# Both hidden-dimension transforms by seven half-size products per pair of row blocks, behind all query and key products

## The chip, the cores and the metric

The kernel runs on one core of one Trainium2 chip. Its time is device time in microseconds (us). Before the change three runs took 851.29, 848.71 and 847.14 us; the median is 848.71 us. One more execution was profiled: it took 850.56 us, and the profile's span of it is 848.9 us.

A core has a matrix engine (PE in the profile; PEld is its weight load), a vector engine (DVE), an activation engine (ACT), GpSimd (POOL), and SP, which here only issues transfers. All of them run their own instruction list in order.

## What is computed

Two token mixers are computed from the same 2048x512 input `x` and blended by a gate per row. The first is the real part of a two-dimensional discrete Fourier transform, as four dense products; the second is attention in a sliding window of 256 with 32 heads of 16.

```python
a = einsum("bsd,ed->bse", x, dft_hid_re)          # 2048x512 by 512x512
b = einsum("bsd,ed->bse", x, dft_hid_im)
fnet = einsum("ts,bse->bte", dft_seq_re, a) - einsum("ts,bse->bte", dft_seq_im, b)
q, k, v = split(x @ wqkv)                         # 32 heads of 16
p = softmax(where(0 <= i - j < 256, q @ k.T / 4, -1e9))
attn = (p @ v) @ wo
g = sigmoid((x * gate_w).sum(-1))
out = g * fnet + (1 - g) * attn
```

All is float32. A dense product is made of three matrix products on split operands: each operand is a high part plus a low part, and high by high, high by low and low by high are added (`TERMS`). The high part is a cast on ACT, the low part a subtraction on DVE (raw minus high).

## The kernel before

**Two streams on PE.** Attention walks over 128 visits `n` (8 pairs of head groups `G` by 16 query blocks). In a visit stand two score products of `s_pair` (L363; DVE then takes a row maximum of each from PSUM, L367), two transposed score products of `t_pair` (L422; ACT takes the exponential, L425, and POOL masks two triangles of it, L427 and L431), and every fourth visit the product with v of four blocks, `pv` (L445). Scores, transposed scores and `pv` share two PSUM buffers (`ps_a`), so a score product waits until DVE has read the one before it. Between the attention's instructions `fill` (L1070) puts steps of the dense stream, in equal numbers for all visits: those steps that are left are spread over the visits that are left.

**The dense stream.** `dense` (L635) yields one step at a time. `halves64` (L534) works through a list of `Part`s. A step is two matmuls (L527): one on partitions 0 to 63 for the running part, and one on partitions 64 to 127 for the part that began `DELAY` = 6 steps earlier; both have 64 rows of weights and 512 columns and share the matrix array. A part of q, k, v, a or b has 12 steps, and a part of the sequence transform (c) 24. `halves64` has 1,950 steps: 70 parts of 12, 46 of 24, and 6. Each part's result is evicted when its second half ends.

**What sets the order.** PE, ACT, DVE, POOL and SP all run in the order in which the code emits (`manual_schedule`). An action can be put off by a number of steps: `after(n, ...)`, and jobs run one every fourth step (`job`, L159). The parts stand in `order` (L722 to L774): some v parts with q and k of group 0, then q and k of group 1 (8 parts), then 16 parts of b (`ab_part(1, sb)`), then q and k of groups 2 and 3 (16 parts), then 16 parts of a. Each q or k part is evicted into `home`, three buffers used in turn (`hl_tile`), and stored to DRAM as 768 KB (`qk_evict`, L274). Each b block, and the first four blocks of a, goes to DRAM as 256 KB (`ab_evict`, L339); the other twelve blocks of a are split in PSUM straight into their places in SBUF. At the start of the c parts `to_c` (L836) loads the four stored blocks of a back and splits them. Later, c parts with b load its 16 blocks by `next_b` (L804).

## Time and profile before

| what | value |
|---|---|
| median of three runs | 848.71 us |
| profiled execution, its own time | 850.56 us |
| span of it in the profile | 848.9 us |
| granted clock of PE, mean | 0.996 |
| DMA moved in the span | 168.80 MB, mean 199 GB/s |
| steps of `halves64` on PE (L527) | first at 33.5 us, last at 697.2 us |
| stores of q and k (`qk_scr<-home`) | 12.5 us to 258.6 us |
| evictions of b (L342); of a into SBUF (L103) | 120.3 to 264.8 us; 271.0 to 318.5 us |
| last `pv` of the attention (L445) | starts at about 698 us |

The profile's page gives busy times by engine, and the trace answers more narrow questions: groups of instructions by line, waits, single instructions in order of time, and the busy time of each engine in any stretch. One cycle below means four visits of the attention, from the start of one `pv` to the start of the next; it holds 8 pairs of score products and about 58 dense steps.

### The profile page before, as it was taken

Reading aid. Unit: us, or ns where it says so; the run is one execution under the profiler, and the core shown is the slowest. Engines: PE = TensorE matmul, PEld = TensorE weight load, DVE = VectorE, ACT = ScalarE, POOL = GpSimd, SP = SyncE. Lnnn points to the kernel's source line nnn. Section 1 sums busy time; section 2 is a strip of 40 time slices with the busy share of each in tenths; the row PEclk is TensorE's granted clock in tenths of the full one; section 3 lists DMA queues with packets and bytes.
Section 4 is the critical chain, followed back from the end, with each engine's and each line's share of the span. In section 5 each row is a group of like instructions: output and inputs, shape, how many; then the busy total and the mean of one; then the engine's idle time right before and its main releaser. Section 6 shows DMA issues by size and latency. Waiting matters only on the chain.

```text
span 848.9 us, 19774 instructions
## 1 busy us (share of the span) xinstructions
PE 821.5 (97%) x7298; PEld 654.2 (77%) x7298; DVE 531.1 (63%) x1504; ACT 418.0 (49%) x814; POOL 365.0 (43%) x683
## 2 busy tenths in 40 slices
...
GB/s 341 279 207 163 283 247 182 169 181 261 302 263 211 144 124 197 138 175 155 169 142 181 153 192 187 226 231 228 237 230 184 168 180 224 261 213 190 179 111 50
DMA packets 109344, 168.80 MB, mean 199 GB/s; under 512 B 34240, under 2 KB 43968, under 8 KB 109248
## 3 DMA queue, kind: packets, MB, share of 16 engines
...
q8 instruction: 57, 0.93, 0.5%
...
HBM read 107.74 MB, written 59.51 MB: 197 GB/s over the span
## 4 chain that ended last, share of the span: by engine, by line
PE 76%; DMA 8%; DVE 7%; issue 5%; ACT 3%; POOL 1%; SPq 1%; ACTq 0%; DVEq 0%; POOLq 0%
PE d L527 41%; PE o L445 9%; PE dc L580 8%; PE s L363 6%; PE t L1012 5%; PE t L422 4%; DVE junk L367 3%; PE d L567 3%; DMA ring<-qk_scr 2%; DMA raw<-ci 2%; ACT pt L425 1%; DVE lo L156 1%; DMA o_scr<-ev 1%; DVE big L140 1%; DMA stage<-ab_scr 1%
## 5 line engine op out<-in xcount | busy, mean ns | idle before, releaser
L367 DVE CUSTOM_DVE_ANT_0 junk<-s,mask 128x384 f32<-128x384 f32 (+2 forms) x512 | 271.9, 531 | 198.0 <-PE s L363 186.9
L527 PE MATMUL d<-big,hi 64*128 64x512 f32 x1920 | 344.5, 394 | 0.0
L427 POOL TENSOR_SCALAR_AFFINE_SELECT pt<-pt 128x256 f32<-128x256 f32 x256 | 112.3, 439 | 359.4 <-ACT pt L425 280.8
L425 ACT ACTIVATE pt<-t 128x768 f32<-128x768 f32 (+2 forms) x256 | 197.6, 772 | 123.8 <-PE t L422 121.4
L527 PEld LDWEIGHTS d<-big,hi 64*128 64x128 f32 x1920 | 195.5, 187 | 27.0 <-issue 0.6
L527 PE MATMUL d<-big,lo 64*128 64x512 f32 x960 | 206.2, 395 | 0.0
L527 PE MATMUL d<-hi,big 64*128 64x512 f32 x672 | 132.3, 392 | 0.0
L363 PE MATMUL s<-ring,ring 48*128 48x384 f32 (+2 forms) x512 | 99.5, 357 | 12.4 <-DMA ring<-qk_scr 3.7
L527 PEld LDWEIGHTS d<-big,lo 64*128 64x128 f32 x960 | 100.6, 187 | 13.2 <-issue 0.2
L155 ACT CAST hi<-raw 128x512 fp32r<-128x512 f32 x142 | 87.1, 618 | 30.0 <-PE d L527 15.2
L156 DVE TENSOR_TENSOR lo<-raw,hi 128x512 fp32r<-128x512 f32 x110 | 85.4, 777 | 12.9 <-ACT hi L155 12.9
L431 POOL TENSOR_SCALAR_AFFINE_SELECT pt<-pt 128x256 f32<-128x256 f32 x224 | 92.9, 415 | 0.0
L580 PE MATMUL dc<-big,hi 128*128 128x512 f32 x284 | 91.7, 392 | 0.0
L422 PE MATMUL t<-ring,ring 50*128 50x384 f32 (+2 forms) x512 | 87.8, 330 | 1.0 <-ACT pt L425 0.5
L445 PE MATMUL o<-pt,vt 128*32 128x384 f32 (+2 forms) x1408 | 84.3, 386 | 3.9 <-DVE ml L367 3.7
L527 PEld LDWEIGHTS d<-hi,big 64*128 64x128 f32 x672 | 76.8, 186 | 7.4
L363 PEld LDWEIGHTS s<-ring,ring 48*128 48x128 f32 x512 | 53.7, 185 | 37.3 <-issue 10.4
L527 PE MATMUL d<-lo,big 64*128 64x512 f32 x336 | 80.4, 392 | 0.0
L445 PEld LDWEIGHTS o<-pt,vt 128*32 128x32 f32 x1408 | 42.0, 110 | 49.7 <-issue 27.6
L422 PEld LDWEIGHTS t<-ring,ring 50*128 50x128 f32 x512 | 50.7, 185 | 14.5 <-ACT pt L425 2.1
L156 POOL TENSOR_TENSOR lo<-raw,hi 128x512 fp32r<-128x512 f32 x32 | 43.0, 1356 | 40.8 <-ACT hi L155 40.5
L580 PEld LDWEIGHTS dc<-big,hi 128*128 128x128 f32 x284 | 52.3, 188 | 8.7 <-issue 0.2
...
## 6 DMA issues: line engine op xcount, KB each, us to landing
ring<-qk_scr SPq DMA_DIRECT2D x128, 192.0 KB
...
```

The source lines that it names most:

```text
L155: jobs.append(lambda c=c: nc.scalar.copy(hi[:, c], raw[:, c]))
L156: jobs.append(lambda c=c: (nc.gpsimd if FIN else nc.vector).tensor_sub(lo[:, c], raw[:, c], f(hi[:, c])))
L363: nc.tensor.matmul(ps[:, h, :w], ring[0][r, p, j * P:j * P + P], ring[1][r, p, k0:k0 + w], start=True, stop=True)
L367: mark("dve", nc.vector.tensor_tensor_reduce(out=junk[:, :w], in0=ps[:, h, :w], in1=mask[:, WIN - w:], scale=1.0, scalar=3e38, op0=OP.add, ...
L422: nc.tensor.matmul(ps[:, h, :w], ring[1][r, p, q0:q0 + P], ring[0][r, p, q0:q0 + w], start=True, stop=True)
L425: nc.scalar.activation(pt[:, ph, :w], ps[:, :, :w], AF.Exp, scale=-1.0)
L427: nc.gpsimd.affine_select(a, a, pattern=[[0, 2], [1, P]], compare_op=OP.is_ge, fill=0.0, base=0, channel_multiplier=-1)
L431: nc.gpsimd.affine_select(a, a, pattern=[[0, 2], [-1, P]], compare_op=OP.is_gt, fill=0.0, base=0, channel_multiplier=1)
L445: nc.tensor.matmul(o[32 * j:32 * j + 32, (a - 4 * c) * P:(e - 4 * c) * P], v[:, kb % 4, 32 * j:32 * j + 32], PT[G * NB + kb][:, j, (a - kb ...
L527: nc.tensor.matmul(o.ps, lhs[r], rhs[r], start=start, stop=end and o.left == 0, skip_group_check=True)
L580: nc.tensor.matmul(ps, w[a][:, i % 8 * 128:i % 8 * 128 + 128], ab[SC[i]][:, b], start=i == ends[0] and a + b == 0, stop=i == ends[1] and a ...
L1012: nc.tensor.matmul(ps, o[:, a, c], fin(n, b, c), start=start and c == 0 and a + b == 0, stop=c == 1 and a == 1, skip_group_check=True)
```

## The change

**a and b together.** For a pair of row blocks (t, t+4) and the two halves of the features, a and b are the columns of one 256x512 by 512x1024 product: a two-by-two block product in which a's and b's weights are the two column halves. It is computed by seven products instead of eight (the Winograd form of Strassen's scheme). `pair` lists them as seven parts of 6 steps, eight pairs in all, in place of the 32 parts of 12 steps. The sums of weight blocks (`w_sum`, four of them, 1024 columns each) and of input blocks (`x_sums`, four of 256 columns per pair) are made on POOL, the splits of the sums on ACT with DVE or POOL (`w_split`, `x_split`), and the results are put together by additions behind the evictions (`keep`, `p5_mid`, `p6_end`, `fourth`, `p7_end`, `p5_end`). The input is loaded again in another layout (`xp`).

**Order.** q and k of groups 1, 2 and 3 (24 parts) now stand one behind the other ahead of all of a and b; the loads and products of the gate (`gate_load`, `gates`) move into parts 9 to 23. `halves64` has 38 parts of 12, 56 of 6, 46 of 24, and 6 steps: 1,902.

**Places.** Weight blocks and input sums reuse the places of the input tiles. All of b and twelve blocks of a now go through DRAM; `reload` brings the twelve back around the start of the c parts, and only 10, 14, 11 and 15 (`place`) are split into SBUF at once. `SC`, the order in which the c parts take the blocks of a and b, follows from that.

```diff
+AHEAD = 216
+SC = 10, 14, 9, 13, 8, 12, 0, 11, 15, 4, 1, 5, 2, 6, 3, 7
...
-    STAGE = []
-
-    def load_ab(i, sc, into):
-        if not STAGE:
-            t = const.tile([P, 6, 512], F32, name="stage", tag="home")
-            STAGE.extend(t[:, k] for k in range(6))
-        STAGE.append(STAGE.pop(0))
-        raw = STAGE[-1]
+    stage = [f(home[:, 512 * k:512 * k + 512]) for k in range(6)]
+
+    def flat(t):
+        return t.rearrange("p a s -> p (a s)")
+
+    def load_ab(i, sc, dst, into, wait=SPLIT_AB):
...
+        stage.append(stage.pop(0))
+        raw = stage[-1]
         ld_pool(raw, ab_scr[i][sc])
 
         def cast():
-            t = into[sc] = big.tile([P, 2, 512], F32R, name="big")
-            nc.scalar.copy(t[:, 0], raw)
-            after(3, nc.vector.tensor_sub, t[:, 1], raw, f(t[:, 0]))
-        after(SPLIT_AB, cast)
-
-    def ab_evict(i, sb, ps, dst=None):
-        if dst is None:
-            t = ev.tile([P, 512], F32, name="ev")
-            nc.scalar.activation(t, ps, AF.Copy, scale=1.0 if i == 0 else -1.0)
-            after(STORE, ld, ab_scr[i][sb], t)
-        else:
-            split_psum(dst[:, 0], dst[:, 1], ps)
-
+            into[sc] = dst
+            nc.scalar.copy(dst[:, 0], raw)
+            after(3, nc.vector.tensor_sub, dst[:, 1], raw, f(dst[:, 0]))
+        after(wait, cast)
...
-        def __init__(self, end, parts=1, load=None):
-            self.end, self.left, self.load, self.ps, self.r = end, 2 * parts, load, None, None
+        def __init__(self, end, parts=1, load=None, mid=None):
+            self.end, self.left, self.load, self.ps, self.r, self.mid = end, 2 * parts, load, None, None, mid
+
+    class Straight(list):
...
-            if o.left:
+            if o.left == 2 and o.mid:
+                o.mid(o)
+            elif o.left:
...
-        second = [(p, i) for g in groups for p in [g[-1], *g[:-1]] for i in range(p.n)]
+        second = [(p, i) for g in groups for p in (g if isinstance(g, Straight) else [g[-1], *g[:-1]])
+                  for i in range(p.n)]
...
-        def ab_part(i, sb, pre=None):
-            def end(o):
-                if i == 0 and sb >= 4:
-                    ab[sb] = big.tile([P, 2, 512], F32R, name="big")
-                ab_evict(i, sb, o.ps, ab.get(sb) if i == 0 else None)
-            return Part(Out(end), lambda: row_ops(sb, W["ab", i]), pre=pre)
...
+        order = [q02, k02, v_part(6), v_part(7), v_part(8), q03, v_part(9), k03, *(v_part(sb) for sb in range(10, 16))]
+        order += [p for ss in range(4) for p in qk_parts(1, ss)]
+        order += [p for ss in range(4) for g in (2, 3) for p in qk_parts(g, ss)]
...
+        def split_to(n, hi, lo, raw, scale=1.0):
+            def high(c):
+                if scale == 1.0:
+                    nc.scalar.copy(hi[:, c], raw[:, c])
+                else:
+                    nc.scalar.activation(hi[:, c], raw[:, c], AF.Copy, scale=scale)
+
+            def low(c):
+                if scale == 1.0:
+                    nc.vector.tensor_sub(lo[:, c], raw[:, c], f(hi[:, c]))
+                else:
+                    nc.vector.scalar_tensor_tensor(lo[:, c], raw[:, c], scale, f(hi[:, c]),
+                                                   op0=OP.mult, op1=OP.subtract)
+            for k, c in enumerate(HALVES):
+                after(n + 6 * k, high, c)
+                after(n + 6 * k + 3, low, c)
...
+        def w_sum(n, op, dst, a, b):
+            def go(c):
+                getattr(nc.gpsimd, op)(RAWS[dst][:, c], RAWS[a][:, c], RAWS[b][:, c])
+            for k, c in enumerate(HALVES):
+                after(n + 2 * k, go, c)
...
+        def x_load(p):
+            RAWS["x", p] = load_raw(xp[p])
+
+        def x_sums(p):
+            r = RAWS["s", p] = raw_tile()
+            a11, a12, a21, a22 = quarters(RAWS["x", p], 4)
+            s3, s1, s2, s4 = quarters(r, 4)
+            nc.gpsimd.tensor_sub(s3, a11, a21)
+            nc.gpsimd.tensor_add(s1, a21, a22)
+            nc.gpsimd.tensor_sub(s2, s1, a11)
+            nc.gpsimd.tensor_sub(s4, a12, s2)
+
+        XSPOTS = [(k, 2) for k in range(4)] + [(k, 3) for k in range(2)]
...
+        def x_split(n, p, k):
+            def go():
+                t = tiles[p, k] = XT[XSPOTS[(4 * p + k) % 6]]
+                m = 256 if k == 3 else 512
+                raw = (RAWS["x", p][:, :512], RAWS["s", p][:, :512],
+                       RAWS["s", p][:, 512:], RAWS["x", p][:, 768:])[k]
+                nc.scalar.copy(t[:, 0, :m], raw)
+                after(3, (nc.gpsimd if k in (1, 2) else nc.vector).tensor_sub, t[:, 1, :m], raw, f(t[:, 0, :m]))
+            after(n, go)
+
+        def prepare():
+            t = AHEAD
+            for n, k, src in ((-190, "i1", wi[1]), (-178, "i0", wi[0]), (-166, "r0", wr[0]), (-100, "r1", wr[1])):
+                after(t + n, load_w, k, src)
+            w_split(t - 144, "b11", "r0", None)
+            w_sum(t - 144, "tensor_sub", "i1", "i0", "i1")
+            w_sum(t - 139, "tensor_add", "i0", "i0", "r0")
+            w_sum(t - 132, "tensor_add", "r0", "i1", "r0")
+            w_split(t - 127, "t3", "i1", None)
+            w_split(t - 105, "t1", "i0", ((0, 1), 0), -1.0)
+            w_split(t - 93, "t2", "r0", ((2, 3), 0))
+            after(t - 84, load_w, "n1", wi[1])
+            w_split(t - 60, "b21", "r1", ((0, 1), 1))
+            w_sum(t - 46, "tensor_sub", "r1", "r1", "r0")
+            w_split(t - 38, "t4", "r1", ((2, 3), 1))
+            w_split(t + 2, "b22", "n1", None, -1.0)
+            for p in range(8):
+                b = t + 42 * p - 42
+                after(t - 38 if p == 0 else t + 14 if p == 1 else b - 8, x_load, p)
+                after(b + (20 if p == 0 else 29 if p == 1 else 22), x_sums, p)
+                for k, n in enumerate((30, 35, 40, 38) if p == 1 else (26, 31, 39, 35)):
+                    x_split(b + n, p, k)
...
+        def pair_rows(p):
+            t = p % 4 + p // 4 * 8
+            return t, t + 4
+
+        def x_ops(p, k, quarter, w):
+            t = tiles[p, k]
+            a = [t[:, h, 256 * quarter:256 * quarter + 256] for h in range(2)]
+            return [(a[i][:, c * 128:c * 128 + 128], WO[w][j][:, c * 512:c * 512 + 512])
+                    for c in range(2) for i, j in TERMS]
+
+        def pair(p):
+            t1, t2 = pair_rows(p)
+            U, V = [], []
...
+            def p5_mid(o):
+                nc.vector.tensor_add(V[0], o.ps, V[0])
+
+            def p6_end(o):
+                nc.vector.tensor_add(U[0], o.ps, U[0])
+
+                def fourth():
+                    nc.gpsimd.tensor_add(V[0], V[0], U[0])
+                    after(STORE, ld, ab_scr[1][t2], V[0])
+                after(3, fourth)
+
+            def place(t, k):
+                ab[t] = XT[((2, 3), (3, 3))[k]] if p == 6 else XT[XSPOTS[(26 + k) % 6]]
+                return ab[t]
+
+            def p1_end(o):
+                if p < 6:
+                    e = ev.tile([P, 512], F32, name="ev")
+                    nc.scalar.copy(e, o.ps)
+                    after(STORE, ld, ab_scr[0][t1], e)
+                else:
+                    d = place(t1, 0)
+                    split_psum(d[:, 0], d[:, 1], o.ps)
+
+            def p7_end(o):
+                e = ev.tile([P, 512], F32, name="ev")
+                nc.vector.tensor_add(e, o.ps, U[0])
+                if p < 6:
+                    after(STORE, ld, ab_scr[0][t2], e)
+                else:
+                    d = place(t2, 1)
+                    after(3, nc.scalar.copy, d[:, 0], e)
+                    after(6, nc.vector.tensor_sub, d[:, 1], e, f(d[:, 0]))
+
+            def p5_end(o):
+                e = ev.tile([P, 512], F32, name="ev")
+                nc.vector.tensor_add(e, o.ps, U[0])
+                after(STORE, ld, ab_scr[1][t1], e)
+
+            o1 = Out(shortly(p1_end), 2, mid=keep(U))
+            o7 = Out(shortly(p7_end), 2, mid=keep(V))
+            o5 = Out(shortly(p5_end), 2, mid=shortly(p5_mid))
+            o6 = Out(shortly(p6_end))
+            return Straight(Part(o, lambda args=args: x_ops(p, *args), 6) for o, *args in
+                            ((o1, 0, 0, "b11"), (o7, 1, 0, "t3"), (o5, 1, 1, "t1"), (o6, 2, 0, "t2"),
+                             (o1, 0, 1, "b21"), (o7, 3, 0, "t4"), (o5, 2, 1, "b22")))
...
-        order += [p for ss in range(4) for p in qk_parts(1, ss, (PRE.get((1, ss)), None))]
-        order += [ab_part(1, sb, do(*AB1.get(sb, ()))) for sb in range(16)]
-        for g in (2, 3):
-            order += [p for ss in range(4) for p in qk_parts(g, ss, (PRE.get((g, ss)), None))]
-        order += [ab_part(0, sb, do(*AB0.get(sb, ()))) for sb in range(16)]
-        groups = [order[:4], *(order[i:i + 3] for i in range(4, len(order), 3))]
...
+        def reload():
+            w = [XT[dk, ss] for ss in range(2) for dk in range(4)]
+            x = [XT[XSPOTS[(28 + k) % 6]] for k in range(4)]
+            casts = [-5] * 6
+            for n, sc, dst in ((27, 9, w[0]), (29, 13, w[1]), (31, 8, x[1]), (34, 12, w[2]), (37, 0, w[3]), (46, 4, w[4]),
+                               (50, 1, w[5]), (54, 5, x[0]), (60, 2, w[6]), (64, 6, w[7]), (68, 3, x[3]), (72, 7, x[2])):
+                at = max(n - 29, casts[-6] + 5)
+                casts.append(n)
+                after(at, load_ab, 0, sc, dst, ab, n - at)
...
+        for p, k, fn in ((6, 1, pieces.load), (7, 0, lambda: (reload(), pieces.load())), (7, 1, pieces.split),
+                         (7, 3, pieces.load), (7, 4, pieces.split), (7, 6, pieces.load)):
+            pairs[p][k].pre = fn
+        groups = [order[:4], *(order[i:i + 3] for i in range(4, 31, 3)), order[31:35], order[35:], *pairs]
...
-        def to_c():
-            for sc in range(4):
-                after(8 * sc, load_ab, 0, sc, ab)
-
-        c_groups[0][0].mid[12] = to_c
...
+        "xp": x.reshape(2, 2, 4, P, 2, 2, P).transpose(0, 2, 6, 1, 4, 5, 3).reshape(8, P, 1024),
```

**What it moves on POOL.** First POOL's instructions before, from the stretch with the parts of b: the two masks of each transposed score product (`pt`), `o_mul` (L475) once in four visits, and a load of the gate's input (L70).

```order
L475 TENSOR_TENSOR ev_2024<-ots_312,ev_2024 128x512
L427 AFFINE_SELECT pt_2162<-pt_2162 128x2x128
L431 AFFINE_SELECT pt_2162<-pt_2162 128x2x128
L427 AFFINE_SELECT pt_2255<-pt_2255 128x2x128
L431 AFFINE_SELECT pt_2255<-pt_2255 128x2x128
L70 DMA raw_2301<-x 128x512 x2
```

And now POOL's list in one of the pairs (lines are those of the changed kernel: L420 and L424 are the masks, L468 is `o_mul`).

```order
L748 TENSOR_TENSOR raw_4019<-raw_3862 128x256
L749 TENSOR_TENSOR raw_4019<-raw_3862 128x256
L750 TENSOR_TENSOR raw_4019<-raw_4019,raw_3862 128x256
L751 TENSOR_TENSOR raw_4019<-raw_3862,raw_4019 128x256
L420 AFFINE_SELECT pt_3989<-pt_3989 128x2x128
L424 AFFINE_SELECT pt_3989<-pt_3989 128x2x128
L468 TENSOR_TENSOR ev_3908<-ots_324,ev_3908 128x512
L72 DMA raw_4076<-xp 128x1024
L142 TENSOR_TENSOR big_491<-raw_4019,big_491 128x512
L816 TENSOR_TENSOR ev_3999<-ev_3999,ev_3969 128x512
L142 TENSOR_TENSOR big_505<-raw_4019,big_505 128x512
```

Between the masks there now stand, for every pair, four sums (L748 to L751), two low parts (L142), one addition of results (L816) and one load; two further pairs of masks stand between the rows of this piece.

**What it moves on DVE.** DVE before, where `to_c` reloaded blocks of a: `junk` and `ml` are the row maxima of a score product, two of each per product; `lo` is the low part of a weight piece, and `big<-stage` that of a reloaded block.

```order
L367 ISA junk_299,ml_4713<-s_4781,mask_287 128x384
L140 TENSOR_TENSOR big_4775<-stage_4641,big_4775 128x512
L140 TENSOR_TENSOR big_4806<-stage_4641,big_4806 128x512
L367 ISA junk_299,ml_4713<-s_4817,mask_287 128x384
L156 TENSOR_TENSOR lo_4809<-raw_4602,hi_4808 128x512
L367 ISA junk_299,ml_4713<-s_4872,mask_287 128x384
L140 TENSOR_TENSOR big_4849<-stage_4641,big_4849 128x512
L156 TENSOR_TENSOR lo_4809<-raw_4602,hi_4808 128x512
```

DVE now, in the last pair and its `reload` (L360 is the row maximum, L142 with `home` a reloaded block, L158 a weight piece, L813, L835 and L845 additions of results, L109 the low part of a block of a that stays, L368 and L369 a small step of the attention).

```order
L142 TENSOR_TENSOR big_278<-home_323,big_278 128x512
L813 TENSOR_TENSOR ev_4441<-d_4500,ev_4441 128x512
L142 TENSOR_TENSOR big_283<-home_323,big_283 128x512
L158 TENSOR_TENSOR lo_4524<-raw_4368,hi_4523 128x512
L142 TENSOR_TENSOR big_593<-home_323,big_593 128x512
L360 ISA junk_311,ml_4288<-s_4583,mask_299 128x384
L142 TENSOR_TENSOR big_286<-home_323,big_286 128x512
L368 CAST mlh_4609<-ml_4288 128x4x16
L369 TENSOR_TENSOR mlh_4609<-ml_4288,mlh_4609 128x4x16
L142 TENSOR_TENSOR big_293<-home_323,big_293 128x512
L109 TENSOR_TENSOR big_505<-d_4370,big_505 128x512
L360 ISA junk_311,ml_4623<-s_4624,mask_299 128x384
```

The next gap between two score products holds five again.

```order
L158 TENSOR_TENSOR lo_4524<-raw_4368,hi_4523 128x512
L835 TENSOR_TENSOR ev_4635<-d_4402,ev_4441 128x512
L142 TENSOR_TENSOR big_522<-ev_4635,big_522 128x512
L142 TENSOR_TENSOR big_394<-home_323,big_394 128x512
L845 TENSOR_TENSOR ev_4664<-d_4438,ev_4441 128x512
L360 ISA junk_311,ml_4623<-s_4669,mask_299 128x384
```

Where two row maxima had at most two other instructions of 512 columns between them, three gaps in a row now hold five, three and five. (The second row maximum of each product and the short rows that read an accumulator are left out.)

108 lines of the change are left out of this document (55 added, 53 removed).

## The prediction

> **What bounds the kernel now.** The page's first block and its chain of waits name the engine: PE is busy nearly all the time and holds three quarters of the chain that ends last.
>
> ```profile
> PE 821.5 (97%) x7298; PEld 654.2 (77%) x7298; DVE 531.1 (63%) x1504; ACT 418.0 (49%) x814; POOL 365.0 (43%) x683
> ...
> PE 76%; DMA 8%; DVE 7%; issue 5%; ACT 3%; POOL 1%; SPq 1%; ACTq 0%; DVEq 0%; POOLq 0%
> ```
>
> DVE's 63% and POOL's 43% are averages, and this change puts all its new work into one third of the span. So the second view is the busy time by cycle, each cut at the starts of two `pv`. The columns are PE, PEld, DVE, ACT and POOL busy, the granted clock, the DMA share and GB/s.
>
> ```profile
> 109.38:129.46 20.08, 19.29 (x196) 15.36 (x196) 13.16 (x41) 10.99 (x23) 9.83 (x21) 1.00 0.80 255
> 129.46:148.59 19.13, 19.13 (x201) 14.98 (x199) 10.80 (x39) 9.98 (x22) 7.34 (x16) 1.00 0.57 183
> ...
> 187.21:210.92 23.71, 21.37 (x198) 17.84 (x196) 13.18 (x41) 11.04 (x23) 8.36 (x19) 0.93 0.86 275
> ...
> 270.87:293.70 22.83, 20.27 (x199) 15.23 (x197) 16.77 (x49) 12.24 (x24) 11.31 (x23) 1.00 0.46 125
> 293.70:313.51 19.81, 19.42 (x196) 16.15 (x197) 14.07 (x43) 10.03 (x22) 7.08 (x15) 1.00 0.46 128
> ...
> 506.86:526.21 19.35, 19.35 (x199) 15.00 (x197) 12.25 (x40) 11.37 (x21) 8.34 (x19) 1.00 0.69 209
> ...
> 611.34:631.79 20.45, 19.31 (x196) 14.90 (x196) 17.07 (x45) 10.63 (x23) 9.26 (x19) 1.00 0.86 245
> ```
>
> A cycle in which PE never rests takes 19.13 us (b parts) or 19.35 us (c parts, with PE busy 19.35 of it): there the dense steps set the time. A cycle with DVE at 17.07 us lost 1.1 us against that. The two worst, 23.71 and 22.83, hold waits of PE for transfers: the view of PE's waits lists one of 2.0 us for a store of q or k, and two, 3.7 us together, for ring loads.
>
> ```profile
> PE s L363 <- DMA ring<-qk_scr: 3.7, 2, 2.3
> ...
> PE s L363 <- DMA qk_scr<-home: 2.0, 1, 2.0
> ```
>
> **The change part by part.** The sum is made against the profiled execution (span 848.9 us, its own time 850.56). That execution lies 1.9 us above the median of 848.71, so the difference found here is put on the median.
>
> *Steps removed.* The price of a step is read from the list of single instructions in a stretch without waits (start, length, and how many matmuls stand in the row).
>
> ```profile
> 680.39 0.63 PE L527 MATMUL d<-big,hi 64*128 64x512 f32 x4
> 680.86 0.39 PE L527 MATMUL d<-big,lo 64*128 64x512 f32 x2
> 681.09 0.62 PE L527 MATMUL d<-big,hi 64*128 64x512 f32 x4
> 681.55 0.40 PE L527 MATMUL d<-big,lo 64*128 64x512 f32 x2
> 681.78 0.34 PE L422 MATMUL t<-ring,ring 50*128 50x384 f32 x2
> ```
>
> From 680.39 to 681.78 twelve matmuls start, six steps: 0.232 us a step (a row's length overlaps the next one). The 32 parts of b and a have 384 steps, the 56 new parts 336, in matmuls of the same shape. 48 steps x 0.232 = **-11.1 us**. `fill` spreads the 1,902 steps over the same visits, so a cycle has some 56 steps where it had some 58, and a quiet one takes about 19.35 - 1.3 x 0.232 = 19.05 us. A pair's 42 steps take 42/56 of that, 14.3 us.
>
> *POOL beside the pairs.* The rows give number, minimum, median and maximum in ns.
>
> ```profile
> L427 POOL TENSOR_SCALAR_AFFINE_SELECT pt<-pt x256: 396/406/918, 71.6 to 696.7; 128x256 f32<-128x256 f32 x128
> ...
> L475 POOL TENSOR_TENSOR ev<-ots,ev x32: 1263/1292/1823, 126.3 to 724.9; 128x512 f32<-128x512 f32 x32
> ...
> L975 POOL TENSOR_TENSOR ex<-ex,tw x5: 730/742/1189, 719.4 to 790.6; 128x256 f32<-128x256 f32 x5
> ...
> L156 POOL TENSOR_TENSOR lo<-raw,hi x32: 1262/1299/1746, 701.8 to 827.5; 128x512 fp32r<-128x512 f32 x32
> ...
> L70 POOL DMA_DIRECT2D stage<-ab_scr x20: 553/556/577, 321.4 to 631.4; - x20
> ```
>
> A pair puts on POOL four sums of 256 (4 x 0.742), two low parts and one addition of 512 (2 x 1.299 + 1.292) and one load (0.556): 7.4 us. The attention's share of 14.3 us is twelve masks (12 x 0.406) and three quarters of an `o_mul` (0.97): 5.8 us. Sum 13.3 of 14.3 us, **93%** at the medians. What covers it: a mask is needed late. At 411.30 a `pv` starts whose last mask ended 3.0 us before.
>
> ```profile
> 407.87 0.40 POOL L431 TENSOR_SCALAR_AFFINE_SELECT pt<-pt 128x256 f32<-128x256 f32 x1
> ...
> 411.30 2.15 PE L445 MATMUL o<-pt,vt 128*32 128x384 f32 x32 [0.18 <-DVE ml L367]
> ```
>
> The four sums in a row, 3.0 us, just fit, and the first reader of the sums stands nine steps (about 3 us) behind their issue and needs the first two of them. I cost this at **+1 us**. If the cover is gone, each pair takes what POOL takes; at the maxima of the rows (4 x 1.189 + 2 x 1.746 + 1.823 + 0.577 + 5.8) that is 16.4 us, 2.1 us more for each of eight pairs. So the bounds are 0 and +17, and I stay near the lower since the medians leave 1 us of air.
>
> *DVE beside q, k and the pairs.* The price of its instructions, then two score products of a quiet stretch with the first maximum of each (the others of DVE are left out), then DVE's time in L367 in one cycle:
>
> ```profile
> L107 DVE TENSOR_TENSOR home<-d,home x15: 677/690/693, 28.8 to 253.0; 128x512 fp32r<-128x512 f32 x15
> ...
> L156 DVE TENSOR_TENSOR lo<-raw,hi x110: 627/686/2115, 61.2 to 694.3; 128x512 fp32r<-128x512 f32 x110
> ...
> 513.69 0.34 PE L363 MATMUL s<-ring,ring 48*128 48x384 f32 x2
> 515.68 0.34 PE L363 MATMUL s<-ring,ring 48*128 48x384 f32 x2
> ...
> 514.07 0.56 DVE L367 CUSTOM_DVE_ANT_0 junk<-s,mask 128x384 f32<-128x384 f32 x1 [0.23 <-PE s L363]
> 516.06 0.56 DVE L367 CUSTOM_DVE_ANT_0 junk<-s,mask 128x384 f32<-128x384 f32 x1 [0.22 <-PE s L363]
> ...
> 506.86:526.21 19.35, 9.06 (x32) 1.00 0.69 209
> ```
>
> Score products follow each other in 1.99 us (1.96 with fewer steps between them; `pv` makes up the rest of a cycle). Maxima start 0.38 us after the product and take 9.06/8 = 1.13 us. Some 0.83 us are left in a gap, one instruction of 512 columns and a bit; the next product waits once more than 0.45 us of lag have piled up, since it needs the maxima of the one before. In a pair stand four additions, a low part of 512 and one of 256 (0.42 by length): gaps of 0.69, 1.38, 1.11, 0.69, and two almost empty ones. Followed from product to product, that makes PE wait 0.1 and 0.3 us. Eight times 0.4 is 3.2; in about half of the pairs a `pv` of 2 to 3 us falls between and takes it up: **+1.5 us**. Bounds: 0, and six cycles at the 1.1 us of row 611.34, so +6.6. Beside q and k the weights' splits rise from 8 to 14 instructions of 512 columns, and the gate's products come earlier, so that some gaps hold three: **+1 us**; 0 below, above it five cycles at 1.1, +5.5.
>
> *The reload.* Here the order on DVE shows gaps with five, three and five instructions of 512 columns. I follow them by hand with the same numbers. Product 0 starts at 0, its maxima end at 1.51. Five instructions end at 4.96 and the maxima of product 1 at 6.09; product 2, wanted at 3.92, waits 2.2. Three and two short ones (2.5 us) take the maxima of product 2 to 9.7; product 3, wanted at 8.05, waits 1.7. Five more: 14.3 against 11.7, 2.6. The list goes on with two in a gap and then three, which a `pv` that is due there covers. Together **+6.5 us**. The upper bound adds the low clock that follows such waits: the cycle 187.21 lost 23.71 - 19.35 = 4.4 us for a wait of 2.0; two waits of that size here, so +11. The lower is 0, if the work falls due later than it is listed. I take the walk, because it needs only durations that hardly vary.
>
> *What goes.* Splitting twelve blocks of a from PSUM made cycles like 293.70, which took 19.81, 0.5 more than 19.35; the stretch of a and the old reload is four cycles long: **-2 us**. The waits for transfers at 199 and 288 us I leave as they are: q and k are still stored part after part, 768 KB each, and ring loads still pass SP in order. DMA grows by 4.2 MB of `xp`, 2 MB of stores and 2 MB of reloads, and 2.5 MB of gate input move beside the parts of group 1, at 255 GB/s in row 109.38 (share 0.80). Those parts take some 32 us, so +78 GB/s; that would bring the share to about 1. I cost it at 0 with bounds of -4.4 (a wait gone) and +9 (two more). ACT gets four casts, three copies and seven short copies a pair:
>
> ```profile
> L155 ACT CAST hi<-raw x142: 606/619/637, 58.3 to 826.8; 128x512 fp32r<-128x512 f32 x142
> ...
> L530 ACT COPY tick<-d x125: 150/159/164, 36.7 to 690.5; 128x1 f32<-128x1 f32 x125
> ```
>
> That is at most 7 x 0.62 + 7 x 0.16 = 5.5 us on top of three quarters of the 9.98 in row 129.46: 13.0 of 14.3, hidden by PE as long as none of them waits.
>
> Sum: -11.1 + 1 (POOL) + 1.5 + 1 (DVE) + 6.5 (reload) - 2 = **-3.1**, so the median goes from 848.7 to about **845.5 us**.
>
> **The rivals.**
>
> *The whole saving comes through.* If the reload's instructions find DVE ahead of PE, or their blocks' loads arrive later and spread them, the 6.5 us vanish: -9.6, 839.1 us. For it: in quiet cycles DVE idles 7 us of 19. Against it: the five stand in one list, and DVE takes them in order.
>
> *POOL and DVE in each other's way.* The trace shows a low part on DVE that stretched to 1.61 us beside a product on POOL; alone it takes 0.69.
>
> ```profile
> 349.64 1.30 POOL L475 TENSOR_TENSOR ev<-ots,ev 128x512 f32<-128x512 f32 x1
> ...
> 349.88 1.61 DVE L156 TENSOR_TENSOR lo<-raw,hi 128x512 fp32r<-128x512 f32 x1
> ```
>
> Each pair has two such low parts on DVE, with POOL in sums and products for 7.8 us of 14.3. Half of the sixteen would meet one and lose about 0.9: 7 us on DVE; POOL waits as much the other way, from 93% to about 100%. If the lag then reaches PE, the pairs cost 5 us more: 850.5 us, no change. Against it: two gaps of a pair are almost empty, and masks have 3 us. The Trainium skill's "SBUF — State Buffer", section "Who interferes with whom", gives this as a rule: a VectorE instruction with two SBUF inputs contends with a GpSimd one that reads SBUF, and whichever comes second blocks until the first is done. The trace agrees (the POOL row ends at 350.94, the DVE one 0.55 us after it). By that rule alone the sum would be this rival's.
>
> *Slower: the stores of q and k.* `home` has three buffers, and 24 parts now fill them one behind the other with the gate's loads beside. A store must land within three parts less its 11 steps of delay, about 25 steps or 8.5 us; from there on ACT waits in an eviction, exponentials stand behind it, and PE stops. One such wait before cost the cycle 4.4 us; two more make -3.1 + 8.8 = +5.7, 854.4 us, and three 858.8. For it: the share of 0.86 in that cycle. Against it: eight parts of group 1 at 255 GB/s had no such wait.
>
> *It doesn't do what it says.* PE's list does have 96 matmuls less, and they stand in the stream that bounds; this one I drop.
>
> **How the numbers follow.** A measurement here tells about 0.5% (4.2 us) from no change, so the border is 844.5, close below the forecast. Chances: the sum as it stands 0.38, the whole saving 0.27, POOL against DVE 0.17, stores 0.18. Faster by over 0.5%: the 0.27, and two fifths of the 0.38 for terms that come out smaller: 0.43. Within: the rest of the 0.38 and most of the POOL rival, 0.38. Slower: the stores, and a little of POOL's, 0.19. The range reaches from 836, below the whole saving by three quarters of a wait for a transfer that goes, to 856, two stores late: some 0.07 are left out below and 0.1 above.
>
> **What would show it.** The steps: 3,792 matmuls on the line of `product` instead of 3,888, and quiet cycles of about 19.05 us. POOL: busy 18 us a cycle beside the pairs, and PE's waits for masks still small. DVE: three waits of PE's score products for `ml` of over 1 us each within 15 us around the first c part, and only short ones beside the pairs. Stores: at most one wait of an eviction for `qk_scr<-home`. The prediction is wrong if cycles beside the pairs take over 20 us, if that reload passes without waits, or if new waits for ring loads or `home` show up.

## The result, and the profile after

The changed kernel takes 891.03 us (median of four executions, 883.99 to 892.62), the kernel before 847.92 beside it: a ratio of 1.0486, 95% interval 1.042 to 1.0552. The change makes the kernel slower by 36 to 47 us; the forecast was 845.5, the range 836 to 856. The profiled execution is the fastest of the four (883.99, span 882.3 us).

The first block of the profile's page, and its chain of waits:

```profile
PE 833.7 (94%) x7202; PEld 644.6 (73%) x7202; DVE 578.4 (66%) x1558; ACT 437.5 (50%) x878; POOL 445.7 (51%) x764
...
PE 67%; DVE 11%; DMA 8%; issue 6%; ACT 4%; POOL 2%; SPq 1%; ACTq 0%; DVEq 0%; POOLq 0%
```

PE is busy for 12 us more, on 96 dense matmuls fewer, and its share of the chain falls from 76% to 67%. Where the time went is read from stretches, here of 56 dense steps each (112 matmuls of `product`, L525 after the change). Columns as in the prediction: PE, PEld, DVE, ACT, POOL busy, granted clock, DMA share, GB/s.

```profile
117.19:142.64 25.45, 21.26 (x197) 15.14 (x197) 15.62 (x49) 11.72 (x25) 15.73 (x23) 0.93 0.78 268
...
208.44:233.94 25.50, 22.42 (x197) 15.39 (x195) 18.20 (x42) 12.68 (x29) 16.26 (x28) 1.00 0.44 135
...
258.81:290.99 32.18, 25.27 (x180) 17.47 (x178) 23.04 (x45) 12.19 (x28) 18.85 (x29) 0.84 0.41 129
...
368.59:387.11 18.52, 18.51 (x181) 14.26 (x178) 12.61 (x41) 11.04 (x22) 8.83 (x21) 1.00 0.49 133
...
339.99:368.59 28.60, 23.08 (x195) 17.49 (x197) 24.31 (x56) 14.67 (x30) 13.00 (x24) 0.88 0.63 193
...
183.39:339.99 156.60, 134.16 (x1150) 92.66 (x1146) 105.46 (x267) 81.19 (x189) 105.35 (x170) 0.97 0.53 166
```

From 368.59 to 557 us, in the c parts, 56 steps take 18.5 to 19.4 us: there the change does what was forecast. (Behind that they take 19.2 to 21.0; the kernel before is slower there too, with up to 22.7.) The last row holds six such stretches, the eight pairs (336 steps): 156.60 us, where six quiet ones of 18.75 take 112.5. **The pairs lose 44 us**, the reload behind them (339.99) 10, and one stretch beside q and k (117.19) 6 to 7. The waits of PE in the pairs follow (columns are total, times, longest). The rows of weight loads name more of them, since PE counts as busy while its pipeline drains; but a weight load runs ahead of its matmul, so its waits are longer than what PE loses:

```profile
PEld d L525 <- ACT tick L530: 35.8, 51, 1.7
...
ACT tick L530 <- PE d L525: 11.7, 16, 2.5
...
PEld s L356 <- DVE ml L360: 5.4, 5, 2.6
...
PEld s L376 <- DVE ml L360: 4.1, 2, 3.2
```

What PE lost is counted from the start of one matmul to the start of the next, less a step of 0.232 us. Over all gaps in the pairs that a tick, or a row maximum, ended, this gives 22.5 us for the ticks and 7.7 us for the maxima (`ml`). The granted clock of 0.97 costs some 5 us more (an estimate, 0.03 x 156.6). That is 35 of the 44 us; no wait in the trace was found for the other 9. The largest item stood in no term of the forecast: 51 waits for the `tick`. Two of them in the list of single instructions, each at the end of the first half of a part:

```profile
191.59 0.39 PE L525 MATMUL d<-hi,big 64*128 64x512 f32 x1
191.85 0.16 ACT L530 COPY tick<-d 128x1 f32<-128x1 f32 x1
...
192.06 0.18 PEld L525 LDWEIGHTS d<-big 64*128 64x128 f32 x1 [0.52 <-ACT tick L530]
192.06 0.50 PE L525 MATMUL d<-big 64*128 64x512 f32 x1
...
240.85 0.39 PE L525 MATMUL d<-hi,big 64*128 64x512 f32 x1
240.94 0.39 ACT L418 ACTIVATE pt<-t 128x256 f32<-128x256 f32 x1
241.22 0.40 ACT L403 COPY vt<-vr 128x256 f32<-128x256 f32 x1
241.51 0.17 ACT L530 COPY tick<-d 128x1 f32<-128x1 f32 x1
...
241.73 0.18 PEld L525 LDWEIGHTS d<-hi,big 64*128 64x128 f32 x1 [0.92 <-ACT tick L530]
241.73 0.50 PE L525 MATMUL d<-hi,big 64*128 64x512 f32 x1 [0.49 <-ACT tick L530]
```

When half of a part ends, ACT reads one column of its PSUM tile (the tick), so that the other half, which writes the same tile, is ordered behind the first. A pair's parts have 6 steps, `DELAY` is 6, and `Straight` gives both halves the same order: the second half of a part begins in the step behind the last one of its first half. In the first case ACT has nothing to do: the tick starts 0.26 us behind the matmul, PE goes on 0.21 later, 0.47 us from matmul to matmul in place of 0.23: PE loses 0.24 us where the weight load shows a wait of 0.52. In the second the tick stands in ACT's queue behind an exponential and a copy, and PE starts nothing for 0.88 us, a loss of 0.65. ACT sat waiting for PE ahead of 16 of the ticks in the pairs (second row of the waits); the others stood behind its own work. With ACT always free, 56 ticks would cost 56 x 0.24 = 13 us (an estimate); they cost 22.5. Before, the rotated order had the second half on another part's tile, and the whole trace has no wait of a dense step for a tick.

### The profile page after: what moved, and what is told of

Its sections match the earlier page's. It is cut to its first block, busy times and chain, and to the rows that moved or that the text cites. A ratio compares the mean times of both kernels' runs of the same rounds, so it can differ in the third digit from the quotient of the medians.

```text
span 882.3 us, 19861 instructions
## 1 busy us (share of the span) xinstructions
PE 833.7 (94%) x7202; PEld 644.6 (73%) x7202; DVE 578.4 (66%) x1558; ACT 437.5 (50%) x878; POOL 445.7 (51%) x764
## 4 chain that ended last, share of the span: by engine, by line
PE 67%; DVE 11%; DMA 8%; issue 6%; ACT 4%; POOL 2%; SPq 1%; ACTq 0%; DVEq 0%; POOLq 0%
PE d L525 35%; PE o L438 9%; PE dc L581 8%; PE t L1145 5%; PE s L356 5%; DVE junk L360 4%; PE t L415 3%; PE d L568 2%; DMA qk_scr<-home 2%; DVE big L142 2%; DMA raw<-ci 2%; DMA ring<-qk_scr 2%; ACT pt L418 2%; DVE lo L158 1%; DMA home<-ab_scr 1%
## 5 line engine op out<-in xcount | busy, mean ns | idle before, releaser
L360 DVE CUSTOM_DVE_ANT_0 junk<-s,mask 128x384 f32<-128x384 f32 (+2 forms) x512 | 271.7, 531 | 174.8 <-PE s L356 163.7
L525 PE MATMUL d<-big,hi 64*128 64x512 f32 x1920 | 337.2, 394 | 0.0
L420 POOL TENSOR_SCALAR_AFFINE_SELECT pt<-pt 128x256 f32<-128x256 f32 x256 | 117.9, 461 | 287.5 <-ACT pt L418 221.6
L525 PEld LDWEIGHTS d<-big,hi 64*128 64x128 f32 x1920 | 189.0, 187 | 27.9 <-issue 0.7
L525 PE MATMUL d<-big,lo 64*128 64x512 f32 x960 | 199.9, 394 | 0.0
L356 PE MATMUL s<-ring,ring 48*128 48x384 f32 (+2 forms) x512 | 106.8, 364 | 12.5 <-DVE ml L360 8.6
L525 PE MATMUL d<-hi,big 64*128 64x512 f32 x352 | 97.5, 408 | 10.9 <-ACT tick L530 10.8
L525 PEld LDWEIGHTS d<-big,lo 64*128 64x128 f32 x960 | 96.4, 187 | 13.4
L415 PE MATMUL t<-ring,ring 50*128 50x384 f32 (+2 forms) x512 | 95.1, 332 | 3.9 <-ACT tick L530 3.8
L424 POOL TENSOR_SCALAR_AFFINE_SELECT pt<-pt 128x256 f32<-128x256 f32 x224 | 97.3, 434 | 0.0
L158 DVE TENSOR_TENSOR lo<-raw,hi 128x512 fp32r<-128x512 f32 x102 | 80.7, 791 | 10.1 <-ACT hi L157 9.8
L525 PE MATMUL d<-big 64*128 64x512 f32 x384 | 81.2, 414 | 4.5 <-ACT tick L530 3.0
L525 PEld LDWEIGHTS d<-hi,big 64*128 64x128 f32 x352 | 55.1, 191 | 23.8 <-ACT tick L530 20.3
L525 PEld LDWEIGHTS d<-big 64*128 64x128 f32 x384 | 52.2, 190 | 18.0 <-ACT tick L530 15.6
L158 POOL TENSOR_TENSOR lo<-raw,hi 128x512 fp32r<-128x512 f32 x32 | 43.0, 1354 | 42.5 <-ACT hi L157 42.3
```

The costliest lines, as they stand in the source:

```text
L158: jobs.append(lambda c=c: (nc.gpsimd if FIN else nc.vector).tensor_sub(lo[:, c], raw[:, c], f(hi[:, c])))
L356: nc.tensor.matmul(ps[:, h, :w], ring[0][r, p, j * P:j * P + P], ring[1][r, p, k0:k0 + w], start=True, stop=True)
L360: mark("dve", nc.vector.tensor_tensor_reduce(out=junk[:, :w], in0=ps[:, h, :w], in1=mask[:, WIN - w:], scale=1.0, scalar=3e38, op0=OP.add, ...
L415: nc.tensor.matmul(ps[:, h, :w], ring[1][r, p, q0:q0 + P], ring[0][r, p, q0:q0 + w], start=True, stop=True)
L420: nc.gpsimd.affine_select(a, a, pattern=[[0, 2], [1, P]], compare_op=OP.is_ge, fill=0.0, base=0, channel_multiplier=-1)
L424: nc.gpsimd.affine_select(a, a, pattern=[[0, 2], [-1, P]], compare_op=OP.is_gt, fill=0.0, base=0, channel_multiplier=1)
```

## The experiments

Each run beside executions of the kernel before on the same chip; four executions of each (e13 ten), compared by their ratio to before.

| run | us | ratio to before, 95% |
|---|---|---|
| the changed kernel | 891.0 | 1.0486 (1.0420 to 1.0552) |
| e1 lag 9 | 890.2 | 1.0498 (1.0473 to 1.0523) |
| e2 lows on POOL | 884.7 | 1.0426 (1.0394 to 1.0458) |
| e3 lag 9, lows on POOL | 886.1 | 1.0448 (1.0425 to 1.0472) |
| e4 gate over a quarter | 891.1 | 1.0514 (1.0466 to 1.0562) |
| e5 lag 9, in place | 883.6 | 1.0424 (1.0366 to 1.0482) |
| e6 lag 9, store from POOL | 894.8 | 1.0539 (1.0483 to 1.0596) |
| e7 lag 9, both of these | 887.5 | 1.0481 (1.0419 to 1.0542) |
| e8 weight loads apart | 891.6 | 1.0514 (1.0455 to 1.0573) |
| e9 gaps in POOL's runs | 892.8 | 1.0518 (1.0453 to 1.0583) |
| e10 as e5, with gaps | 881.6 | 1.0386 (1.0340 to 1.0432) |
| e11 as e5, POOL light | 871.6 | 1.0274 (1.0206 to 1.0342) |
| e12 POOL light | 884.4 | 1.0421 (1.0372 to 1.0470) |
| e13 before, lag 9 | 850.7 | 1.0038 (1.0012 to 1.0065) |
| e14 lag 9 in the pairs only, in place | 881.4 | 1.0388 (1.0340 to 1.0436) |
| e15 as e14, no lows on DVE | 869.3 | 1.0247 (1.0202 to 1.0293) |
| e16 as e15, POOL light | 859.6 | 1.0134 (1.0075 to 1.0192) |
| e17 as e16, lag 6, not in place | 881.3 | 1.0373 (1.0324 to 1.0422) |
| e18 as e16, no lows at the reload | 858.8 | 1.0110 (1.0053 to 1.0166) |

### The tick alone (e1), and DVE behind POOL alone (e2, e9)

The first theory (T) is the tick. The second (S) is that instructions of DVE with two inputs in SBUF wait through POOL's runs. It came from rows like these of the changed kernel, DVE and POOL in the worst stretch:

```profile
283.76 5.36 DVE L142 TENSOR_TENSOR big<-raw,big 128x256 fp32r<-128x256 f32 x1
...
284.00 1.29 POOL L142 TENSOR_TENSOR big<-raw,big 128x512 fp32r<-128x512 f32 x1
...
285.25 1.29 POOL L816 TENSOR_TENSOR ev<-ev 128x512 f32<-128x512 f32 x1
...
286.49 0.40 POOL L420 TENSOR_SCALAR_AFFINE_SELECT pt<-pt 128x256 f32<-128x256 f32 x1
...
287.23 1.25 POOL L142 TENSOR_TENSOR big<-raw,big 128x512 fp32r<-128x512 f32 x1
...
288.80 0.58 POOL L424 TENSOR_SCALAR_AFFINE_SELECT pt<-pt 128x256 f32<-128x256 f32 x1
...
290.25 0.45 PE L356 MATMUL s<-ring,ring 48*128 48x384 f32 x2 [2.34 <-DVE ml L360]
```

A low part of 256 columns, which takes 0.41 us at best, ends at 289.12, 0.26 us ahead of the end of POOL's unbroken run; the maxima stand behind it, and PE waits 2.34 us.

```diff
-DELAY = 6
+DELAY = 9                                          # e1
...
-                for k, n in enumerate((30, 35, 40, 38) if p == 1 else (26, 31, 39, 35)):
+                for k, n in enumerate((30, 35, 43, 38) if p == 1 else (26, 31, 42, 35)):
...
-after(3, (nc.gpsimd if k in (1, 2) else nc.vector).tensor_sub, ...
+after(3, nc.gpsimd.tensor_sub, ...                  # e2
...
+            nc.gpsimd.memset(padt, 0.0)             # e9, behind each sum, low part, fourth addition
```

> The second half of every step runs 9 steps behind the first in place of 6 (and one split per pair is due 3 steps later). Theory T (tick): in the pairs the second half of a part enters the same PSUM tile right behind the first half's last matmul, with ACT's short copy (the tick) between; the changed kernel's weight loads waited 35.8 us for ticks beside the pairs. With three steps (0.7 us) of room these waits fall below 8 us and the time falls by 22 to 34 us against the changed kernel's 884 to 892. A new wait of up to 0.5 us per pair, for the copy that frees the first product's PSUM tile, is allowed for. Theory S (DVE starved behind POOL) alone: the waits for the tick are a symptom of engines that run late; the time stays within 5 us of the changed kernel.

> The two low parts per pair that DVE took (two inputs in SBUF) go to POOL too; nothing else changes. Theory S: a DVE instruction with two SBUF inputs waits through a whole unbroken run of POOL's work (4.5 and 5.4 us seen), then PE waits for the maxima (9.8 us beside the pairs) and runs at half clock behind it (137 slow matmuls); with the lows gone from DVE both vanish, 12 to 18 us less. Theory P (POOL overloaded): POOL's list grows from 13.3 to 15.3 us of a pair's 14.3, masks come late, the time grows by 8 us or more. Theory T alone: no change within 5 us.

> The changed kernel, with a memset of eight columns on POOL, into a tile nobody reads, behind each sum, each low part and each fourth addition (seven a pair). It adds work to POOL and takes none away. Theory S' (DVE's instruction with two SBUF inputs, or a cast there, is let in only where POOL pauses its reading): a memset that only writes is such a pause; the three low parts of 4.5 to 5.4 us fall to 2.1 us or less, PE's waits for the maxima beside the pairs fall from 9.8 to about 3 us, and the time by 8 to 15 us; the ticks' 36 us on the weight loads stay. If only an idle POOL lets DVE in, the long low parts stay and the time is the same or up to 8 us longer.

e1 brought the ticks' waits from 35.8 to 10.8 us, not below 8 as forecast, and the time stayed: theory T, as a single cause, missed by 20 us or more. Its waits from 183 to 385 us, in the pairs and the reload:

```profile
PEld s L356 <- DVE ml L360: 14.5, 9, 4.3
...
PEld d L525 <- ACT tick L530: 10.8, 4, 4.7
...
ACT ev L805 <- DMA ab_scr<-ev: 8.4, 3, 4.2
```

The waits for the maxima grew (9.7 us in the same stretch of the changed kernel), the four that are left for ticks are long (ACT itself waits for stores out of `ev` and the tick stands behind), and low parts of 5.30, 4.88 and 5.38 us are still there. e2 took the low parts from DVE and came out between the theories, 0.6% below the changed kernel with overlapping intervals: its weight loads still wait 36.7 us for ticks, and a small instruction was shut out in place of the large one. Its DVE and POOL:

```profile
262.82 0.60 POOL L72 DMA_DIRECT2D raw<-xp  x1
263.11 5.92 DVE L369 TENSOR_TENSOR mlh<-ml,mlh 128x64 fp32r<-128x64 f32 x1
263.44 1.29 POOL L142 TENSOR_TENSOR big<-raw,big 128x512 fp32r<-128x512 f32 x1
264.68 1.30 POOL L816 TENSOR_TENSOR ev<-ev 128x512 f32<-128x512 f32 x1
...
268.91 0.40 POOL L424 TENSOR_SCALAR_AFFINE_SELECT pt<-pt 128x256 f32<-128x256 f32 x1
```

64 columns, which take 0.23 us in the median, took 5.92. e9 put a write of 0.10 us between POOL's readers:

```profile
286.51 5.53 DVE L142 TENSOR_TENSOR big<-raw,big 128x256 fp32r<-128x256 f32 x1
286.77 1.29 POOL L142 TENSOR_TENSOR big<-raw,big 128x512 fp32r<-128x512 f32 x1
288.01 0.10 POOL L142 MEMSET padt<- 128x8 f32 x1
288.07 1.29 POOL L823 TENSOR_TENSOR ev<-ev 128x512 f32<-128x512 f32 x1
```

The low part still takes 5.53 us: such a pause does not let DVE in, and the time is the same.

### Other waits that e1 shows: transfers, tiles, SP (e3 to e8)

e3 put e1 and e2 together.

> Both edits. If T and S are two separate causes, the gains add: 36 to 50 us below the changed kernel, 838 to 852 us. If POOL is overloaded, this is slower than the kernel with the lag alone by 5 us or more.

It took 886.1: the gains do not add, and neither reading of the sum holds. In e1, SP's own queue stood 42.7 us behind POOL's `fourth` addition, whose store it issues (35.0 in the changed kernel), and ACT's evictions waited 13.0 us for stores out of the five `ev` tiles.

```profile
SPq L69 <- POOL ev L816: 42.7, 7, 11.1
```

```diff
-                e = ev.tile([P, 512], F32, name="ev")          # e5, p5_end
-                nc.vector.tensor_add(e, o.ps, U[0])
-                after(STORE, ld, ab_scr[1][t1], e)
+                nc.vector.tensor_add(U[0], o.ps, U[0])
+                after(STORE, ld, ab_scr[1][t1], U[0])
...
-                    after(STORE, ld, ab_scr[1][t2], V[0])      # e6, fourth
+                    after(STORE, ld_pool, ab_scr[1][t2], V[0])
```

> On the kernel with the lag of 9: the last output of a pair is added into U's tile, which nobody needs any more, so that a pair takes four tiles of the pool of five (ev) in place of five. In the kernel with the lag alone ACT waited 13.0 us for stores out of these tiles (ab_scr and o_scr from ev), with PE's ticks behind it in ACT's queue (9.3 us on PE). Theory E (too few ev tiles): both fall below 3 us, and the time falls by 8 to 14 us against that kernel's 890. Theory B (SP stands behind one store that waits for POOL): the waits move to other tiles, the time changes by less than 4 us.

> On the kernel with the lag of 9: the store of a pair's fourth output, which waits for POOL's addition, is issued by POOL and not by SP. In the kernel with the lag alone SP's queue stood still for 42.7 us behind that addition (7 times, up to 11.1 us), with stores out of ev, ring loads and the row sums' transfers behind it. Theory B: these waits are gone, the ev tiles come free in time, and the time falls by 8 to 15 us against 890. Theory E: the tiles are too few in any case, 0 to 5 us less. Theory S (DVE behind POOL) alone: no change; POOL gets 0.56 us a pair more.

> Lag of 9, the addition in place and the store from POOL together. If tick, ev tiles and SP's queue are what costs beside the pairs, the pairs' stretch (eight stretches of 56 steps from about 184 us) falls from 25 to 20 or 21 us each, and the time to 845 to 860. If DVE behind POOL is a cause of its own, PE's waits for the maxima stay at 10 us or more and the time at 865 to 880.

Only the tile did anything: 883.6 against e1's 890.2 is less than theory E gave, the two intervals overlap a little, and ACT still waited 5.7 us for stores out of `ev`. Issuing the store from POOL took SP's wait for the addition away altogether, and the time did not fall (894.8; e7 887.5). SP then stood 46.4 us behind transposed products (17.0 in e1), so the wait for the addition did not set the time. e7 missed both of its theories.

The stretch at 117 to 143 us has a cause of its own: an eviction of q or k finds its place in `home` still being stored, ACT stops, and PE behind it. The changed kernel:

```profile
129.49 0.60 ACT L105 ACTIVATE home<-d 128x512 fp32r<-128x512 f32 x1 [4.81 <-DMA qk_scr<-home]
```

e4 loads and multiplies the gate's input over 128 of 512 columns; e8 moves three weight loads apart:

```diff
-            ld_pool(GX[j][:, HALVES[c]], x[2 * j + c])
+            ld_pool(GX[j][:, 512 * c:512 * c + 128], x[2 * j + c][:, :128])     # e4
...
-... (-190, "i1", wi[1]), (-178, "i0", wi[0]), (-166, "r0", wr[0]), (-100, "r1", wr[1])):
+... (-190, "i1", wi[1]), (-168, "i0", wi[0]), (-146, "r0", wr[0]), (-88, "r1", wr[1])):   # e8
```

> The gate's input is loaded and multiplied over 128 of its 512 columns only: 1.9 MB of loads beside group 1's q and k are left out, and 0.4 us of DVE in each of 16 gate products. Theory H (transfers): the eviction that waited 4.8 us for a store of q or k at 124.7 us waited because loads of gate input and weights and the stores shared the queues; its wait falls below 1 us and the 56 steps that took 25.45 us take 19.5 to 20.5, so 5 to 6 us less in all. If the weights' loads alone fill the queues there, the wait stays and the time changes by less than 2 us.

> The changed kernel, with the loads of i0, r0, r1 and the work on them 10 to 22 steps later, so that the three weight loads of 0.5 MB that stood within 7 us at 114 to 121 us come 7 us apart. Theory H2: the store that landed 13.6 us after its issue (115.8 to 129.4 us), for which an eviction waited 4.8 us, was late because these loads shared the queues; the wait falls below 1 us, the 56 steps of 25.45 us take 19.5 to 21, and the time falls by 4 to 6 us. If the stores and ring loads alone fill the queues, it stays within 2 us.

With a quarter of the gate's bytes the wait is nearly whole (4.0 us, first row); with the weight loads apart it is 2.1 us and comes later (second row). The 56 steps from 116.73 us then take 20.3 us, but the next 56 take 24.5 instead of 21.1, perhaps because the sums and splits of the weights moved along with their loads. So these loads take part in that wait, and the time as a whole does not show it.

```profile
ACT home L105 <- DMA qk_scr<-home: 4.0, 1, 4.0
```

```profile
ACT home L105 <- DMA qk_scr<-home: 2.1, 1, 2.1
```

### Two limits side by side (e10 to e17)

e10 to e12 tried to relieve POOL and DVE with and without the tick; "light" leaves out a pair's four sums on POOL and its fourth addition. A version that leaves work out no longer computes the product; it only prices that work.

```diff
-            r = RAWS["s", p] = raw_tile()                     # light: e11, e12, e16, e17, e18
-            a11, a12, a21, a22 = quarters(RAWS["x", p], 4)
-            s3, s1, s2, s4 = quarters(r, 4)
-            nc.gpsimd.tensor_sub(s3, a11, a21)
...
+            RAWS["s", p] = RAWS["x", p]
...
-                    nc.gpsimd.tensor_add(V[0], V[0], U[0])
...
+        at = min(k for k, e in enumerate(second) if e[0] is straight[0])          # e14 to e16, e18
+        second[at:at] = [None] * MORE                    # MORE = 3
+        at = max(k for k, e in enumerate(first) if e[0] is straight[-1]) + 1
+        first[at:at] = [None] * MORE
...
-                after(3, (nc.gpsimd if k in (1, 2) else nc.vector).tensor_sub, ...  # e15 to e18
+                if k in (1, 2):
+                    after(3, nc.gpsimd.tensor_sub, ...
```

> The kernel with the lag of 9 and the addition in place (883.6), with the same memsets. Theory S': its long DVE instructions beside the pairs (5.0, 4.6, 3.3 and 5.4 us) fall to 2.1 us or less; since the ticks' waits are gone here too, the time falls by 15 to 25 us to 858 to 868. If only an idle POOL lets DVE in: 880 to 892.

> The kernel with the lag of 9 and the addition in place; the four sums of a pair on POOL are left out (the products read x itself in their place), and so is the fourth addition: 4.3 us of POOL less in each pair of 14.3. Theory Q (POOL's list is the root: runs that shut DVE out, masks and SP's stores late behind it): no DVE instruction beside the pairs takes over 2.1 us, cycles there take 19 to 20.5 us in place of 25, and the time is 842 to 855. If ACT or the ev tiles hold the pairs up by themselves, cycles stay at 22 us or more and the time above 865.

> The changed kernel (lag 6) with the same sums and additions left out. Theory T (the tick costs by itself): the weight loads still wait 25 us or more for ticks beside the pairs and the time stays at 868 or above. If the ticks were late only because everything else was, they fall below 10 us and the time lies within 5 us of the kernel with the lag and without the sums.

e10 repeated what e9 had shown. e11 fell to 871.6, short of what theory Q gave: four low parts on DVE still took 3.9 to 4.4 us each beside the shorter runs of POOL. e12 stayed near the changed kernel with 34.5 us of tick waits. So each seemed to count only where the other was gone. e13 asked whether the lag of 9 costs something of its own outside the pairs.

> The kernel before with a lag of 9 in place of 6, nothing else. With the lag of 9 the stretches of 56 steps behind the pairs took 0.1 to 1.5 us longer each (504.9 us from the end of the pairs to the end, 494.8 in the changed kernel). Theory L: the lag itself costs this where parts are 12 or 24 steps long, and hides what it gains in the pairs: this kernel takes 855 to 862, against 848 for before. If the loss came from the pairs' leftovers, it takes 846 to 850.

It does, but little: 0.4%, some 3 us, not the 7 to 14 that theory L gave. e14 therefore has it in the pairs alone, with the addition in place, and e15 to e17 fill the table.

> The changed kernel with the lag of 9 within the pairs alone (three empty steps of the second half ahead of them, three of the first half behind them), and the addition in place. Theory T with L: the ticks' waits beside the pairs (36 us on the weight loads) fall below 8 us without the cost elsewhere: 868 to 876, 15 to 22 us below the changed kernel. If the pairs are held up by other work in any case: 880 or more.

> The kernel with the lag in the pairs alone and the addition in place; the two low parts per pair on DVE (512 and 256 columns) are left out, POOL's work stays whole. Theory S: the DVE instructions of 4 to 5.4 us go with them, PE's waits for the maxima beside the pairs fall below 5 us, cycles there take 19.5 to 21.5: 856 to 864. If casts and small differences of the row maxima's split are shut out instead (5.0 and 5.9 us seen where POOL had the lows), one or two such waits remain: 862 to 870. If DVE's sheer load counts, and not POOL: 9 us less at most (8 times 1.1 us of DVE), and the long instructions move to the next two-input one.

> As the one before, and POOL's four sums and the fourth addition of each pair are left out too. If tick, ev tiles and DVE behind POOL together make up the loss beside the pairs, the seven stretches of 56 steps there take 19 to 20 us, and the time is 846 to 854; what is left then is the stretch at 117 to 143 us and the reload. If it stays above 862, a cause has not been found.

> The changed kernel as it is (lag of 6, five ev tiles a pair) with what e16 leaves out: DVE's two low parts, POOL's four sums and the fourth addition of each pair. Theory T' (the tick is the floor of the pairs with the lag of 6, whatever else goes): the weight loads wait 28 to 36 us for ticks beside the pairs, the stretches of 56 steps there stay at 23 to 25 us, and the time is 876 to 884, 17 to 25 above e16's 859.6. If the ticks were late only because ACT, DVE and POOL were, they fall below 10 us and the time is 858 to 864.

| us; the pairs' six stretches | all of DVE's and POOL's work | no low parts on DVE, POOL light |
|---|---|---|
| tick on PE's path (lag 6) | 891.0; 156.6 | 881.3 (e17); 153.1 |
| tick out of the way (lag 9, in place) | 881.4 (e14); 151.1 | 859.6 (e16); 131.2 |

Either one alone is worth some 10 us, with intervals that still overlap the changed kernel's a little; the second one, once the other is gone, 22, well clear of the intervals. The columns differ in DVE's low parts and POOL's load at once (e15 stands between them), the rows in the lag and the addition in place. The pairs of e17, then of e14, then of e16:

```profile
183.36:336.48 153.12, 134.33 (x1149) 94.30 (x1146) 83.89 (x252) 81.31 (x188) 72.48 (x132) 0.96 0.55 172
```

```profile
184.27:335.38 151.11, 127.47 (x1150) 98.04 (x1150) 107.67 (x265) 81.32 (x187) 104.39 (x168) 0.92 0.54 168
```

```profile
187.44:318.62 131.18, 119.82 (x1150) 95.58 (x1150) 82.68 (x250) 79.73 (x185) 71.64 (x131) 0.97 0.64 198
```

In e17 the ticks stay. With 33 us of POOL's work and 22 of DVE's gone, ACT has as much to do as before (81.31 us against 81.19), and PE's weight loads wait as long for the tick as ever:

```profile
PEld d L525 <- ACT tick L530: 36.6, 53, 1.8
```

Counted at PE's starts this is 22.3 us, against 22.5 in the changed kernel and 4.3 in e16: some 18 of the 22 us between e17 and e16. So theory T' holds: relieving DVE and POOL takes nothing off the ticks. The addition in place does not explain the gain: e17's pairs hold 7.7 us of waits for stores out of `ev` (2.4 on ACT, 5.3 on DVE), e16's 7.3. In e14 most of the ticks' cost is gone, and the other limit shows:

```profile
PEld s L357 <- DVE ml L361: 13.1, 6, 4.3
...
PEld s L377 <- DVE ml L361: 5.5, 2, 4.1
PEld d L526 <- ACT tick L531: 5.3, 4, 2.5
```

At PE's starts the ticks fall from 22.5 to 4.4 us, but the waits for the maxima rise from 7.7 to 16.3, and the granted clock of the pairs falls from 0.97 to 0.92, by an estimate another 7 us (0.08 x 151.1 less 0.03 x 156.6): fewer but longer waits give back most of what the ticks took, and the pairs gain 5.5 us. The time of 881.4 fits e14's second reading, that other work holds the pairs up. Leaving out DVE's two low parts a pair is then worth 12 us (e15): the waits for the maxima fall to 4.1 us, and the clock is back at 0.96. POOL's 4.3 us a pair are worth 10 more (e16). e15 fell within the range for small instructions shut out in place of large ones, and it has one: a cast of 64 columns, in the split of the row maxima, took 5.3 us. e16 fell between its two readings: its pairs still take 131 us, 19 more than quiet ones, in waits for other engines of which none is over 6 us in all.

### The reload (e18)

e18 leaves out the low parts of the twelve blocks that are loaded back.

```diff
-            after(3, nc.vector.tensor_sub, dst[:, 1], raw, f(dst[:, 0]))
+            if i:
+                after(3, nc.vector.tensor_sub, dst[:, 1], raw, f(dst[:, 0]))
```

> As e16, and the low parts of the twelve blocks of a that are loaded back (twelve instructions of DVE with two inputs) are left out too. In e16 the two stretches of 56 steps around the reload took 22.7 and 25.5 us, 10.6 more than twice 18.8. Theory D (DVE's low parts of the reload, lengthened beside POOL to 0.89 and 1.78 us, hold the score products up): both take 18.8 to 20 us, the time falls by 7 to 10 us to 850 to 853. If the loads or ACT's casts hold it up, it changes by less than 3 us.

The stretch around the reload in e16, and then in e18:

```profile
318.62:346.52 27.90, 23.41 (x198) 16.93 (x196) 24.86 (x60) 15.60 (x34) 12.52 (x24) 0.88 0.68 202
```

```profile
316.46:341.03 24.57, 20.61 (x199) 15.04 (x196) 15.67 (x48) 15.38 (x33) 11.22 (x23) 1.00 0.76 225
```

DVE has 9 us less to do and the stretch is 3.3 us shorter, not 7 to 10; ACT now waits 6.0 us for the blocks themselves (`home<-ab_scr`, four times). The times, 859.6 and 858.8, do not tell the two kernels apart. The time fits the second reading, that loads or casts hold the reload up; the stretch by itself shows that DVE's low parts lengthen it too. What sets the rest is open.

## Why the prediction was wrong

**The step that failed** is the end of "What goes": the ticks were priced as ACT's time (7 x 0.16 us a pair, "hidden by PE as long as none of them waits"). What an order list shows, and was not asked of it, is who stands on either side of the tick: in a pair it lies between two matmuls into one tile that stand in neighbouring steps. The sum needed one more term, 56 x (time from the last matmul's start to ACT's reading, the copy, the way back, less one step), and the time that a tick stands in ACT's queue, which was put at 91% of a pair in the same sentence. The first stood in rows that the prediction quotes: a product's first reader starts 0.38 us behind it, and a tick takes 0.159; less a step of 0.232 that is 0.3 us a part, an estimate of 17 us, more than all gains of the sum. Measured it is 0.24 us with ACT free and 0.4 on average (22.5 by 56), and some 18 of the 22 us between e17 and e16, where the other limit is gone.

**Steps.** Right: the rows on `product`'s line hold 3,792 matmuls, and cycles from 378 to 547 us hold 55 or 56 steps and take 18.8 us on average (forecast 19.05). Beside the pairs they take 25 to 30 us, which the prediction had named as a sign of being wrong.

**POOL and DVE.** The mechanism of the rival was right, its price was not. It gave 0.9 us for half of the low parts and 5 us in all, taking one POOL instruction as the obstacle. The runs show whole unbroken runs of POOL's list as the obstacle, 4.5 to 5.9 us at a time, and small instructions hit like large ones. From e14 to e16, where DVE's low parts and 4.3 us of POOL's work a pair are left out, the time falls by 22 us; that bounds the rival's price from above, since the work's own time goes too. The terms +1 and +1.5 for POOL and DVE in the pairs are mis-sized by the same. That POOL would be busy 18 us of a cycle beside the pairs was about right (16.3 and 18.9 in two stretches of 56 steps); that masks wait without harm held too.

**Stores of q and k.** Forecast at 0, with a rival that priced one wait at 4.4 us. One came (4.81 us), and its stretch took 25.45 us. The weight loads bear on it (e8), gate input hardly (e4). The prediction's reading of the waits before was off in one place, without effect on the sum: its "two worst" cycles are not the worst. The one from 526.21 to 550.50 took 24.29 us and holds 2.3 of the 3.7 us of waits for ring loads.

**Reload.** Forecast +6.5 with DVE as the cause. The mechanism came as forecast: three waits for the maxima, 4.2 us in place of 6.5.

```profile
PEld s L356 <- DVE ml L360: 4.2, 3, 2.4
```

The stretch lost 10 us in the changed kernel (28.60 against 18.75), more than these waits. Its granted clock of 0.88 is worth 3.4 us by an estimate (0.12 x 28.60); the prediction had the low clock in its upper bound alone. In e16 the stretch lost 9, and e18 puts about a third of that on DVE's low parts.

**What is left.** e16 lies 1.3% above the kernel before, 14 us above the forecast, with 19 us lost in the pairs, 9 at the reload and 7 beside q and k still in it, against the 11 that the steps save. No version here beats the kernel before.
